# Attention and a gated feed-forward layer on one core: the q, k, v loads change queue, the fallback path is rewritten, the last two output tiles change engine

## The chip, the cores and the metric

The kernel runs on one core of a Trainium2 chip. The core has a matrix engine (TensorE, PE in the profile), three elementwise engines (VectorE or DVE, ScalarE or ACT, GpSimd or POOL) and a sync engine (SyncE, SP) that issues transfers. Each engine works through its own list of instructions in order, and semaphores tie the lists together. Transfers between device memory and the on-chip buffers run on 16 shared DMA engines; an engine that issues one puts it on its own queue (SP's, ACT's, or POOL's, which the profile calls q1, q10 and q0). The metric is the device time of one execution in microseconds (us).

## The reference

Eight batches with eight heads, 1152 keys and a head size of 64. Queries are averaged in pairs, so that there are 576 of them per head; then comes ordinary softmax attention. Its 4608 x 512 result goes through a feed-forward layer in which two projections are multiplied:

```
q_pool = q.reshape(B, H, S // 2, 2, D).mean(axis=3)
attn   = softmax(q_pool @ k^T / sqrt(D))
x      = (attn @ v)            # to 4608 x 512
out    = ((x @ w1) * (x @ w2)) @ w3 @ w_out
```

## The kernel before

**Staging.** The 64 heads are handled as 32 pairs `p` (two heads share the 128 partitions). For each pair, k, q and v are loaded as float32 (`load_kq`, lines 206 to 209, and `load_v`, lines 211 to 215), POOL casts k and v and adds neighbouring queries (`cast_kq`, `cast_v`, lines 228 to 236), and the cast block `kq16` is transposed into `kqT`: on PE for pairs 0 to 7 (`transp_pe`), by a transposing transfer on SP's queue from pair 8 on (`transp`, line 243). `kst`, `qst`, `qtl` and `vst`, the landing buffers, have two copies each, `kq16` two, `kqT` three, `vaugs` six.

**Attention.** `scores(s)` computes 512 columns of the scores of both heads on PE (line 301), and ACT takes the exponential into a ring buffer (line 306). No maximum is subtracted. `av_unit` multiplies 128 query rows with v (line 363), DVE takes the reciprocal of the sum and scales (lines 368, 375), and the result goes to `xT`, transposed on PE for early pairs and by a transfer on SP's queue for pairs from 8 on (`x_dma`, line 320).

**Feed-forward.** `w3 @ w_out` is formed once. Chunks of 512 rows of `xT` go through steps `a` and `b` (lines 459, 472, 474) and `o` (line 453), which gives an output tile `osb` of 128 x 512 (three buffers). While attention still runs, DVE scales that tile and POOL's queue stores it (line 483). After the last score (`tail`), DVE scales the first half and ACT the second, and SP stores it (lines 478 to 480). The next to last tile goes to ACT's queue. The last tile is made in two column halves by `fill_last` (lines 497 to 510): DVE scales the first, ACT the second, and ACT's queue stores both.

**What sets the order.** The string `PLAN` is the order of PE's work, written out by hand: `s` a score slot, `a` and `c` units of attention times v, `f`, `F` and `D` feed-forward steps, `k`, `j` and `t` transposes. The other engines' lists follow from it. When the scores reach a new pair `pn`, `slot` (lines 587 to 600) issues the transposing transfer of pair `pn + 1` and `prepare(pn + 2)`: POOL casts k and q of that pair, casts v of the pair before it, and then come the loads of v of that pair and of k and q of the pair two later. `eng` in line 574 says from which queue: POOL's below pair 8, SP's from there on. Since queues are served in order, whatever waits at the head of POOL's list (a store waiting for its tile, say) holds the casts behind it, and whatever waits at the head of SP's list (an `x_dma` waiting for DVE, a load waiting for its buffer) holds the transposes behind it.

**The fallback.** As no maximum is subtracted, the kernel counts reciprocal sums that are out of bounds (`count_bad`, `read_bad`). All engines read that count (line 668) and branch on it (line 670): if it is not zero, `_general` computes everything again in a plain loop over batches. With the given inputs it is zero and every engine jumps over that code to its end, but the code is there in each engine's list: the loop's body is unrolled over the heads.

Of the kernel before, what the change touches and what calls it, by code (L numbers as in the profile page):

```python
# [8 lines left out]
FP32 = mybir.dt.float32  # L9
FP16 = mybir.dt.float16  # L10
AF = mybir.ActivationFunctionType
ALU = mybir.AluOpType
# [14 lines left out]
def _general(tc, q, k, v, out, w1sb, w2sb, T16):  # L27

    nc = tc.nc
    B, H, S, D = q.shape  # L30
    Sq = S // 2
    NJ = S // 128
    dm = H * D
# [8 lines left out]
    kf, qf, vf = (t.rearrange("b h s d -> (b h) s d") for t in (k, q, v))  # L42
    with tc.tile_pool(name="gen", bufs=1) as sb, \
         tc.tile_pool(name="gen_ps", bufs=1, space=bass.MemoryType.PSUM) as ps, \
         tc.For_i(0, B, 1) as ib:
        xT = sb.tile([128, NC, Sq], FP16)
        for h in range(H):
            ih = ib * H + h
            hs = (h % 2) * 64
            kst = sb.tile([128, NJ, D], FP32, tag="g_kst")  # L50
            nc.sync.dma_start(out=kst, in_=kf[bass.ds(ih, 1)].rearrange("o (c p) d -> p (o c) d", p=128))
            vst = sb.tile([128, NJ, D], FP32, tag="g_vst")
            nc.sync.dma_start(out=vst, in_=vf[bass.ds(ih, 1)].rearrange("o (c p) d -> p (o c) d", p=128))
            qst = sb.tile([QP, QC, 2, D], FP32, tag="g_qst")
            nc.sync.dma_start(out=qst, in_=qf[bass.ds(ih, 1)].rearrange("o (c p t) d -> p (o c) t d", p=QP, t=2))
            kh = sb.tile([128, NJ, 128], FP16, tag="g_kh")
            qh = sb.tile([QP, QC, 128], FP16, tag="g_qh")
            vh = sb.tile([128, NJ, D], FP16, tag="g_vh")
            nc.vector.memset(kh, 0.0)
            nc.vector.memset(qh, 0.0)  # L60
            nc.vector.tensor_copy(out=kh[:, :, 0:D], in_=kst)
            nc.vector.tensor_tensor(out=qh[:, :, 0:D], in0=qst[:, :, 0, :], in1=qst[:, :, 1, :], op=ALU.add)
            nc.vector.tensor_copy(out=vh, in_=vst)
            kT = sb.tile([128, NJ, 128], FP16, tag="g_kT")
            nc.sync.dma_start(out=kT, in_=kh.rearrange("p c d -> p (c d)"), transpose=True)
            qT = sb.tile([128, QC, QP], FP16, tag="g_qT")
            nc.sync.dma_start(out=qT, in_=qh.rearrange("p c d -> p (c d)"), transpose=True)
            kTf = kT.rearrange("p c i -> p (c i)")
            pav = ps.tile([128, 1024], FP32, tag="g_pav")
            for c in range(QC):  # L70
                pss = ps.tile([128, S // W, 512], FP32, tag="g_pss")
                for w in range(S // W):
                    nc.tensor.matmul(pss[0:QP, w, 0:W], qT[:, c, :], kTf[:, w * W:w * W + W], start=True, stop=True)
# [4 lines left out]
                e = sb.tile([QP, S // W, W], FP32, tag="g_e")  # L78
# [6 lines left out]
                eh = sb.tile([QP, S], FP16, tag="g_eh")  # L85
                nc.vector.tensor_scalar(out=eh, in0=e.rearrange("p w i -> p (w i)"), scalar1=rz, scalar2=SCL,
                                        op0=ALU.mult, op1=ALU.mult)
                eT = sb.tile([128, NJ, QP], FP16, tag="g_eT")
                nc.sync.dma_start(out=eT, in_=eh, transpose=True)
                pc = pav[hs:hs + 64, (c // 5) * 512 + (c % 5) * QP:(c // 5) * 512 + (c % 5) * QP + QP]  # L90
                for jt in range(NJ):
                    nc.tensor.matmul(pc, vh[:, jt, :], eT[:, jt, :], start=(jt == 0), stop=(jt == NJ - 1))
                nc.vector.tensor_copy(out=xT[hs:hs + 64, h // 2, c * QP:c * QP + QP], in_=pc)
# [24 lines left out]
def kernel(  # L118
# [11 lines left out]
    nc = tc.nc  # L130

    B, H, S, D = q.shape
    Sq = S // 2
    NJ = S // 128
# [4 lines left out]
    HP = H // 2  # L139
# [9 lines left out]
    SCL = 16.0  # L149
# [7 lines left out]
    CH = 512  # L157
# [304 lines left out]
    def put(step, pt):  # L462
        kind, c, ft = step
        tail = st["s"] == NS
        if kind == "turn":
            w3T[ft] = msb.tile([128, NF, 128], FP16, tag="w3T", bufs=2, name="w3T")
            nc.vector.tensor_copy(out=w3T[ft].rearrange("p a i -> p (a i)"), in_=pt.bitcast(FP16))
        elif kind == "mult":
            nc.vector.tensor_copy(out=T16[:, ft, :], in_=pt)
        elif kind == "a":  # L470
            asbs[ft] = msb.tile([128, CH], FP32, tag="asb", bufs=2, name="asb")
            (nc.scalar.copy if tail else nc.vector.tensor_copy)(out=asbs[ft], in_=pt)  # L472
# [24 lines left out]
    def fill_last():  # L497
        _, c, n = take()
        osb = msb.tile([128, dm], FP32, tag="osb", bufs=3, name="osb")
        for x in range(2):  # L500
            cs = slice(x * 256, x * 256 + 256)
            pt = double()[:, 0, 0:256]
            for f_ in range(NF):
                nc.tensor.matmul(pt, gTs[c][:, f_, n * 128:n * 128 + 128], T16[:, f_, cs],
                                 start=(f_ == 0), stop=(f_ == NF - 1))
            if x == 0:
                nc.vector.tensor_scalar_mul(out=osb[:, cs], in0=pt, scalar1=1.0 / (SCL * SCL))
            else:
                nc.scalar.mul(out=osb[:, cs], in_=pt, mul=1.0 / (SCL * SCL))
            store(nc.scalar, c * CH + n * 128, osb, cs)  # L510

    def fill_two(banks):
        st["mode"] = 1
# [188 lines left out]
```

## Time and profile before

| what | us |
|---|---|
| median of three runs | 414.12 (414.11 to 414.66) |
| the profiled execution | 416.36 |
| its span, first to last instruction | 414.6 |
| PE busy | 397.8 |
| ACT busy | 323.9 |
| DVE busy | 207.0 |
| POOL busy | 164.6 |

The time of the profiled execution holds 1.76 us outside the span. Busy time counts computing instructions of an engine, and for POOL the making of its transfers. A group row names the line, the engine, what is written and read, how often, the busy time and the mean duration of one in ns; the releaser is what ended the idle time before it. `POOLq`, `SPq` and so on are the sequencers of these engines.

### The profile page before, as it was taken

How to read it: one execution, taken by the hardware profiler on the slowest of the kernel's cores; microseconds unless marked ns; L12 is line 12 of the kernel's file. 1: busy time of each engine (PE TensorE's matmuls, PEld its weight loads, DVE VectorE, ACT ScalarE, POOL GpSimd, SP SyncE). 2: the span in 40 equal slices, each digit the busy share in tenths (PEclk: the TensorE clock that was granted, in tenths of full speed). 3: DMA queues.
4: the chain of work that ended last, by engine and by line, in shares of the span. 5: the costliest groups of instructions: out<-in, count | busy, mean ns of one | idle time of the engine just before them, and what ended most of it. 6: DMA issues, size and time to landing. Idle time of an engine off the chain costs nothing.

```text
span 414.6 us, 12630 instructions
## 1 busy us (share of the span) xinstructions
PE 397.8 (96%) x5273; PEld 233.3 (56%) x5273; DVE 207.0 (50%) x568; ACT 323.9 (78%) x357; POOL 164.6 (40%) x208
## 2 busy tenths in 40 slices
PE   4889999999999999999999999999999999999993
PEld 1547665656456655555556545565687555654442
DVE  2446555656356544564455635554466366454331
ACT  4878988999989999999888898998888977323231
POOL 2879977653173317530564057304443200000000
PEclk9999999999999999999999999999999999999998
DMA  8999999999989959999899989894995622120303
GB/s 262 226 321 278 267 283 307 350 253 272 279 189 237 265 179 239 306 270 262 217 222 281 280 218 296 228 233 95 258 262 115 173 52 15 40 86 4 103 0 108
DMA packets 91359, 86.34 MB, mean 208 GB/s; under 512 B 59680, under 2 KB 65056, under 8 KB 91296
## 3 DMA queue, kind: packets, MB, share of 16 engines
q1 hardware_dynamic: 82000, 59.78, 59.8%
q0 software_dynamic: 8720, 25.10, 21.6%
q8 instruction: 43, 0.70, 0.7%
q10 hardware_dynamic: 576, 0.59, 0.4%
q14 instruction: 20, 0.16, 0.2%
HBM read 67.11 MB, written 9.44 MB: 185 GB/s over the span
## 4 chain that ended last, share of the span: by engine, by line
PE 91%; DMA 6%; DVE 0%; POOL 0%; issue 0%; SPq 0%; ACT 0%; ACTq 0%; DVEq 0%; POOLq 0%
PE one L459 22%; PE psc L301 19%; PE one L363 18%; PE one L453 12%; PE psc L459 9%; PE one L450 3%; PE psc L453 3%; DMA w3c<-in_moe_w_dram 3%; PE one L390 3%; DMA wosb<-in_moe_w_out_dram 2%; DMA kst<-in_k_dram 1%; PE psc L248 1%; PE one L447 1%; PE one L331 0%; PE one L328 0%
## 5 line engine op out<-in xcount | busy, mean ns | idle before, releaser
L306 ACT ACTIVATE ring<-psc 128x1024 f16<-128x1024 f32 x324 | 307.2, 1027 | 41.7 <-PE psc L301 40.9
L301 PE MATMUL psc<-kqT 64*128 64x512 f16 (+7 forms) x1152 | 95.3, 290 | 1.3 <-DVE kqT L251 0.7
L363 PEld LDWEIGHTS <-ring 128*128 128x128 f16 x2304 | 81.2, 98 | 26.4 <-issue 11.4
L363 PE MATMUL one<-vaug,ring 128*128 128x65 f16 x2304 | 90.6, 194 | 0.0
L301 PEld LDWEIGHTS <-kqT 64*128 64x128 f16 x1152 | 43.8, 95 | 39.5 <-issue 20.2
L225 POOL CAST kq<-kst 128x1152 f16<-128x1152 f32 x31 | 35.7, 1152 | 52.3 <-DMA kqT<-kq 31.6
L459 PE MATMUL one<-xT,w1sb 128*128 128x512 f16 (+1 forms) x224 | 53.6, 364 | 0.0
L453 PE MATMUL one<-T,gT 128*128 128x512 f16 x224 | 53.0, 380 | 0.0
L459 PE MATMUL one<-xT,w2sb 128*128 128x512 f16 (+1 forms) x224 | 51.5, 357 | 0.0
L472 DVE COPY asb<-one 128x512 f32<-128x512 f32 x46 | 31.8, 692 | 26.4 <-PE one L459 26.4
L474 DVE TENSOR_TENSOR gT<-one,asb 128x512 f16<-128x512 f32 x50 | 34.6, 692 | 20.7 <-PE one L459 18.6
L430 POOL DMA_DIRECT2D out_dram<-osb x21 | 11.6, 554 | 82.4 <-DVE rzall L368 50.1
L459 PEld LDWEIGHTS <-w2sb 128*128 128x128 f16 x320 | 28.5, 97 | 26.2 <-issue 1.8
L453 PEld LDWEIGHTS <-gT 128*128 128x128 f16 x280 | 25.3, 98 | 31.4 <-issue 4.6
L459 PEld LDWEIGHTS <-w1sb 128*128 128x128 f16 x320 | 27.5, 97 | 25.8 <-issue 3.7
L368 DVE RECIPROCAL rzall<-one 128x2 f32<-128x2 f32 x128 | 21.4, 167 | 40.2 <-PE one L363 29.3
L219 POOL TENSOR_TENSOR kq<-qst 128x512 f16<-128x512 f32 x30 | 38.2, 1273 | 3.3 <-DMA qst<-in_q_dram 3.3
L482 DVE TENSOR_SCALAR osb<-one 128x512 f32<-128x512 f32 x24 | 16.6, 692 | 42.8 <-PE one L453 42.8
L236 POOL CAST vaug<-vst 128x1152 f16<-128x1152 f32 x32 | 36.6, 1144 | 3.1 <-DMA vst<-in_v_dram 3.0
L375 DVE TENSOR_TENSOR xb<-one,rzall 128x128 f16<-128x128 f32 x96 | 28.0, 292 | 3.3
L474 DVE TENSOR_TENSOR gT<-psc,asb 128x512 f16<-128x512 f32 x22 | 15.2, 692 | 15.0 <-ACT asb L472 9.3
L459 PE MATMUL psc<-xT,w2sb 128*128 128x512 f16 (+1 forms) x96 | 22.6, 361 | 0.0
(78 smaller groups left out, 257.0 us busy)
## 6 DMA issues: line engine op xcount, KB each, us to landing
vst<-in_v_dram SPq DMA_DIRECT2D x25, 576.0 KB, 5.3
kst<-in_k_dram SPq DMA_DIRECT2D x23, 576.0 KB, 5.9
qst<-in_q_dram SPq DMA_DIRECT2D x23, 512.0 KB, 6.9
out_dram<-osb POOLq DMA_DIRECT2D x21, 256.0 KB, 5.1
kst<-in_k_dram POOLq DMA_DIRECT2D x8, 576.0 KB, 9.9
qst<-in_q_dram POOLq DMA_DIRECT2D x8, 512.0 KB, 11.2
vst<-in_v_dram POOLq DMA_DIRECT2D x7, 576.0 KB, 7.0
out_dram<-osb SPq DMA_DIRECT2D x9, 256.0 KB, 2.0
```

The lines of the kernel that those rows point to most:

```text
L219: eng.tensor_tensor(out=kq16[:, NJ:NJ + QM].rearrange("p c u d -> p u c d"), in0=qv[:, :, :, 0], in1=qv[:, :, :, 1], op=ALU.add)
L225: nc.gpsimd.tensor_copy(out=kq16[:, 0:NJ].rearrange("p c u d -> p u c d"), in_=kq[p][0])
L236: nc.gpsimd.tensor_copy(out=va[:, :, :, 0:D], in_=vs.pop(p).rearrange("p u (c d) -> p u c d", d=D))
L301: nc.tensor.matmul(psc[:, u, f - s * G:f - s * G + ln], kT2[u * 64:u * 64 + 64, jt, :], qpT[u * 64:u * 64 + 64, i0:i0 + ln], start=True, s ...
L306: nc.scalar.activation(out=ring[:, :, r0:r0 + G], in_=psc, func=AF.Exp, bias=0.0, scale=SCALE)
L363: nc.tensor.matmul(one[:, u * E1:u * E1 + E1], ring[:, u, c0:c0 + 128], va[:, u, jt, :], start=(jt == 0 and u == 0), stop=(jt == NJ - 1), ...
L368: nc.vector.reciprocal(out=rz, in_=av[:, :, D:E1].rearrange("p u o -> p (u o)"))
L375: nc.vector.tensor_tensor(out=xbt, in0=av[:, :, 0:D], in1=rz.unsqueeze(2).to_broadcast([128, 2, D]), op=ALU.mult)
L453: nc.tensor.matmul(pt, gTs[c][:, f_, ft * 128:ft * 128 + 128], T16[:, f_, :], start=(f_ == 0), stop=(f_ == NF - 1))
L459: nc.tensor.matmul(pt[:, d0:d0 + n], wt[:, mc, ft * 128:ft * 128 + 128], xT[:, mc, a:a + n], start=(mc == 0 and d0 == 0), stop=(mc == NC - ...
L472: (nc.scalar.copy if tail else nc.vector.tensor_copy)(out=asbs[ft], in_=pt)
L474: nc.vector.tensor_tensor(out=gTs[c][:, ft, :], in0=pt, in1=asbs.pop(ft), op=ALU.mult)
```

## The change

1. `prepare` takes POOL's queue for the loads of v, k and q of every pair, except v of pair 20, which stays on SP's queue. SP's list keeps the first loads, the transposes and stores at the end.
2. In the tail, the next to last tile is scaled by ACT alone in one 128 x 512 instruction and stored from SP's queue. The last tile has both halves scaled by ACT; the first is stored from SP's queue, the second from ACT's.
3. `_general` loads a whole batch at once, packs two heads into the 128 partitions instead of padding with zeros, and transposes a head's six query blocks in one transfer instead of six. It still isn't executed with these inputs. SP's list, the whole program counted, goes from 255 to 93 rows, DVE's from 951 to 880, ACT's from 40 to 38 (repeated ones in a row counted once), POOL's from 208 to 297; PE's has 12060 in both. Of these the part after the branch, which holds the fallback, has 103 rows before and 28 after on SP, 417 and 348 on DVE; on ACT it holds 48 exponentials both times.

`PLAN` is unchanged. The diff, cut:

```
     def prepare(p):
         cast_kq(p)
         cast_v(p - 1)
-        eng = nc.gpsimd if p < 8 else nc.sync
-        load_v(p, eng)
+        eng = nc.gpsimd
+        load_v(p, nc.sync if p == 20 else eng)
...
             osb = msb.tile([128, dm], FP32, tag="osb", bufs=3, name="osb")
-            if tail:
+            if tail and st["f"] >= len(steps) - 1:
+                nc.scalar.mul(out=osb, in_=pt, mul=1.0 / (SCL * SCL))
+                store(nc.sync, c * CH + ft * 128, osb)
+            elif tail:
                 nc.vector.tensor_scalar_mul(out=osb[:, 0:256], in0=pt[:, 0:256], scalar1=1.0 / (SCL * SCL))
                 nc.scalar.mul(out=osb[:, 256:512], in_=pt[:, 256:512], mul=1.0 / (SCL * SCL))
-                store(nc.scalar if st["f"] >= len(steps) - 1 else nc.sync, c * CH + ft * 128, osb)
+                store(nc.sync, c * CH + ft * 128, osb)
...
-            if x == 0:
-                nc.vector.tensor_scalar_mul(out=osb[:, cs], in0=pt, scalar1=1.0 / (SCL * SCL))
-            else:
-                nc.scalar.mul(out=osb[:, cs], in_=pt, mul=1.0 / (SCL * SCL))
-            store(nc.scalar, c * CH + n * 128, osb, cs)
+            nc.scalar.mul(out=osb[:, cs], in_=pt, mul=1.0 / (SCL * SCL))
+            store((nc.sync, nc.scalar)[x], c * CH + n * 128, osb, cs)
...
 _general:
-            kst = sb.tile([128, NJ, D], FP32, tag="g_kst")
-            nc.sync.dma_start(out=kst, in_=kf[bass.ds(ih, 1)].rearrange("o (c p) d -> p (o c) d", p=128))
+        kst = sb.tile([128, H, NJ * D], FP32, tag="g_kst")
+        nc.sync.dma_start(out=kst, in_=kf[bass.ds(ib, 1)].rearrange("o (x p c) d -> p (o x) (c d)", p=128, c=NJ))
...
-                eT = sb.tile([128, NJ, QP], FP16, tag="g_eT")
-                nc.sync.dma_start(out=eT, in_=eh, transpose=True)
+            eT = sb.tile([128, QC * NJ, QP], FP16, tag="g_eT")
+            nc.sync.dma_start(out=eT, in_=eh.rearrange("p c s -> p (c s)"), transpose=True)
```

More of the change, by code (lines that the diff above doesn't have):

```diff
@@ L41, in _general @@
     W = 384
-    kf, qf, vf = (t.rearrange("b h s d -> (b h) s d") for t in (k, q, v))
+    NW = S // W
+    kf, qf, vf = (t.rearrange("b h s d -> b (h s) d") for t in (k, q, v))
     with tc.tile_pool(name="gen", bufs=1) as sb, \
@@ new lines, in _general @@
+        kst = sb.tile([128, H, NJ * D], FP32, tag="g_kst")
+        nc.sync.dma_start(out=kst, in_=kf[bass.ds(ib, 1)].rearrange("o (x p c) d -> p (o x) (c d)", p=128, c=NJ))
+        vst = sb.tile([128, H, NJ * D], FP32, tag="g_vst")
+        nc.sync.dma_start(out=vst, in_=vf[bass.ds(ib, 1)].rearrange("o (x p c) d -> p (o x) (c d)", p=128, c=NJ))
+        qst = sb.tile([QP, H * QC, 2 * D], FP32, tag="g_qst")
+        nc.sync.dma_start(out=qst, in_=qf[bass.ds(ib, 1)].rearrange("o (c p t) d -> p (o c) (t d)", p=QP, t=2))
@@ new lines, in _general @@
+        kh = sb.tile([128, HP, NJ, 2, D], FP16, tag="g_kh")
+        qh = sb.tile([QP, HP, QC, 2, D], FP16, tag="g_qh")
+        vh = sb.tile([128, H * NJ, D], FP16, tag="g_vh")
+        kv_ = kst.rearrange("p (x u) (c d) -> p x u c d", x=HP, d=D)
+        qv = qst.rearrange("p (x u c) d -> p x u c d", x=HP, u=2)
+        for u in range(2):
+            nc.vector.tensor_copy(out=kh[:, :, :, u, :], in_=kv_[:, :, u])
+            nc.vector.tensor_tensor(out=qh[:, :, :, u, :], in0=qv[:, :, u, :, 0:D], in1=qv[:, :, u, :, D:2 * D], op=ALU.add)
@@ new lines, in _general @@
+        nc.vector.tensor_copy(out=vh, in_=vst.rearrange("p h (c d) -> p (h c) d", d=D))
+        kT = sb.tile([128, HP * NJ, 128], FP16, tag="g_kT")
+        nc.sync.dma_start(out=kT, in_=kh.rearrange("p x c u d -> p (x c u d)"), transpose=True)
+        qT = sb.tile([128, HP * QC, QP], FP16, tag="g_qT")
+        nc.sync.dma_start(out=qT, in_=qh.rearrange("p x c u d -> p (x c u d)"), transpose=True)
+        pav = ps.tile([128, 1024], FP32, tag="g_pav")
+        for h in range(H):
+            hp, hs = h // 2, slice((h % 2) * 64, (h % 2) * 64 + 64)
+            eh = sb.tile([QP, QC, S], FP16, tag="g_eh")
+            for c in range(QC):
+                pss = ps.tile([128, NW, 512], FP32, tag="g_pss")
+                for w in range(NW):
+                    t0 = hp * NJ + w * (NJ // NW)
+                    nc.tensor.matmul(pss[0:QP, w, 0:W], qT[hs, hp * QC + c, :],
+                                     kT[hs, t0:t0 + NJ // NW, :].rearrange("p c i -> p (c i)"), start=True, stop=True)
@@ L77, in _general @@
                 nc.vector.tensor_scalar_mul(out=nb, in0=mx, scalar1=-SCALE)
[L78 removed]
+                e = sb.tile([QP, NW, W], FP32, tag="g_e")
                 nc.scalar.activation(out=e, in_=pss[0:QP, :, 0:W], func=AF.Exp, bias=nb, scale=SCALE)
@@ L84, in _general @@
                 nc.vector.reciprocal(out=rz, in_=z)
[L85 to L86 removed]
+                nc.vector.tensor_scalar(out=eh[:, c, :], in0=e.rearrange("p w i -> p (w i)"), scalar1=rz, scalar2=SCL,
                                         op0=ALU.mult, op1=ALU.mult)
[L88 to L90 removed]
+            eT = sb.tile([128, QC * NJ, QP], FP16, tag="g_eT")
+            nc.sync.dma_start(out=eT, in_=eh.rearrange("p c s -> p (c s)"), transpose=True)
+            for c in range(QC):
+                pc = pav[hs, (c // 5) * 512 + (c % 5) * QP:(c // 5) * 512 + (c % 5) * QP + QP]
                 for jt in range(NJ):
[L92 to L93 removed]
+                    nc.tensor.matmul(pc, vh[:, h * NJ + jt, :], eT[:, c * NJ + jt, :], start=(jt == 0), stop=(jt == NJ - 1))
+            for c0, c1 in ((0, 5), (5, QC)):
+                nc.vector.tensor_copy(out=xT[hs, hp, c0 * QP:c1 * QP], in_=pav[hs, (c0 // 5) * 512:(c0 // 5) * 512 + (c1 - c0) * QP])
         gT = sb.tile([128, NF, Sq], FP16)
```

24 lines of the change are left out of this document (1 added, 23 removed).

## The prediction

> **What bounds the kernel.** I read the page first, then the busy time by stretches, then the chain of waits at the end. Of the page, the span, PE's line, and the shares of the chain that ended last:
>
> ```profile
> span 414.6 us, 12630 instructions
> PE 397.8 (96%) x5273; PEld 233.3 (56%) x5273; DVE 207.0 (50%) x568; ACT 323.9 (78%) x357; POOL 164.6 (40%) x208
> PE 91%; DMA 6%; DVE 0%; POOL 0%; issue 0%; SPq 0%; ACT 0%; ACTq 0%; DVEq 0%; POOLq 0%
> ```
>
> An average of 96% hides where the other 4% are. The view by stretches tells (length; busy time of each engine; clock, DMA share, GB/s):
>
> ```profile
> 0.00:10.00 10.00, 3.86 (x26) 1.69 (x26) 1.80 (x6) 4.59 (x7) 2.72 (x11) 1.00 0.81 259
> 20.00:40.00 20.00, 18.16 (x303) 11.78 (x300) 10.35 (x37) 16.71 (x19) 16.80 (x23) 1.00 1.03 311
> 60.00:80.00 20.00, 20.00 (x303) 12.33 (x301) 11.68 (x36) 18.07 (x20) 14.98 (x20) 1.00 0.98 321
> 200.00:220.00 20.00, 20.00 (x299) 11.90 (x295) 10.76 (x30) 17.52 (x19) 11.37 (x14) 1.00 1.15 224
> 380.00:400.00 20.00, 20.00 (x95) 8.98 (x93) 6.65 (x13) 5.58 (x12) 0.00 (x0) 1.00 0.16 53
> 408.00:414.60 6.60, 0.29 (x3) 0.01 (x1) 0.00 (x0) 0.38 (x1) 0.00 (x0) 0.69 0.28 89
> ```
>
> PE is idle in the ramp, where the change moves nothing (`prepare` used POOL's queue there already), and in the last 6.3 us. Between, in the stretch where the loads change queue, PE has no idle time to give back: 20.00 of 20.00 at full clock. So moving the loads can't gain; it can only cost, or free something at the end. What can gain is the tail. Its rows: the chain, ACT's timeline, and the transfers' own times to landing (the SP rows are the stores issued at 403.99 and 405.7, the ACT rows those at 407.45, 407.97 and 408.82):
>
> ```profile
> 404.81 1.73 PE one L453 x8
> 406.54 0.89 PE psc L504 x8
> 407.97 0.34 ACTq L430
> 408.41 0.38 ACT osb L509
> ```
>
> ```profile
> 407.45 0.85 ACTq L430 DMA_DIRECT2D out_dram<-osb  x2
> 408.41 0.38 ACT L509 ACTIVATE osb<-psc 128x256 f32<-128x256 f32 x1 [0.99 <-PE psc L504]
> 408.82 0.88 ACTq L430 DMA_DIRECT2D out_dram<-osb  x1
> ```
>
> ```profile
> out_dram<-osb SPq DMA_DIRECT2D x1, 256.0 KB, 2.1
> ...
> out_dram<-osb SPq DMA_DIRECT2D x1, 256.0 KB, 2.2
> ...
> out_dram<-osb ACTq DMA_DIRECT2D x1, 256.0 KB, 3.4
> out_dram<-osb ACTq DMA_DIRECT2D x1, 128.0 KB, 3.2
> out_dram<-osb ACTq DMA_DIRECT2D x1, 128.0 KB, 3.5
> ```
>
> PE's last matmul ends at about 408.29 (the 408.00 stretch shows 0.29 us of PE). ACT starts the last scaling at 408.41, issues its store at 408.82, and the store lands 3.5 us later, at 412.3. Here are the instructions of the branch over the fallback, by sequencer:
>
> ```profile
> L670 SPq EVENT_SEMAPHORE  x8: 17/17/17, 412.3 to 412.9; - x8
> L670 PEldq COMPARE_BRANCH  x1: 4282/4282/4282, 406.6 to 406.6; - x1
> L670 SPq COMPARE_BRANCH  x1: 58/58/58, 407.0 to 407.0; - x1
> L670 DVEq COMPARE_BRANCH  x1: 72/72/72, 408.2 to 408.2; - x1
> L670 ACTq COMPARE_BRANCH  x1: 62/62/62, 410.3 to 410.3; - x1
> L670 ACTq EVENT_SEMAPHORE  x1: 17/17/17, 410.8 to 410.8; - x1
> L670 DVEq EVENT_SEMAPHORE  x1: 21/21/21, 412.3 to 412.3; - x1
> ```
>
> SP's closing waits begin at 412.3, when the last store lands, and the rest to 414.6 (2.3 us) is the closing sequence. So the tail is: PE's end 408.29, plus 0.12 until ACT starts, 0.38 of scaling, 0.03 to the issue, 3.5 to the landing, 2.3 to close.
>
> **The change, part by part.**
>
> *Loads to POOL's queue.* 23 loads of v (pairs 8 to 31 without 20) and 22 each of k, q and the q remainder (pairs 10 to 31) go from SP's list to POOL's: 89 transfers. The price of one on POOL, from the eight pairs that already did so, and what POOL waits for longest:
>
> ```profile
> L208 POOL DMA_DIRECT2D kst<-in_k_dram x8: 712/728/746, 12.0 to 71.5; - x8
> L202 POOL DMA_DIRECT2D qst<-in_q_dram x8: 724/724/729, 12.7 to 72.2; - x8
> L203 POOL DMA_DIRECT2D qtl<-in_q_dram x8: 607/607/613, 13.4 to 72.9; - x8
> L214 POOL DMA_DIRECT2D vst<-in_v_dram x7: 726/726/726, 14.0 to 70.8; - x7
> POOL out_dram L430 <- DVE rzall L368: 50.1, 9, 17.3
> ```
>
> One `prepare` gets 0.728 + 0.724 + 0.607 + 0.726 = 2.79 us longer; over all, 23 x 0.726 + 22 x 2.059 = 62 us, so POOL goes from 164.6 to about 227 us, 55% of the span. That is beside PE's work as long as POOL catches up before the next transpose needs its cast. The cover is POOL's waiting at stores: nine waits of 50.1 us in total, one of 17.3 us, each ending when PE finishes an output tile, whatever POOL did before. In the stretch 60 to 80, where POOL issues these loads now, it is 14.98 of 20 us busy and PE does not stop. I take zero. The lower bound is zero as well, since PE has no idle time there. The upper bound comes from the transposes that have least room. For the pairs 15 and 20: issue, us to landing, and PE's group that holds the pair's first score:
>
> ```profile
> 156.18 1.54 SPq L243 DMA_TRANSPOSE kqT<-kq  x1
> kqT<-kq SPq DMA_TRANSPOSE x1, 7.3
> 164.88 0.83 PE L301 MATMUL psc<-kqT 64*128 64x384 f16 x10
> ...
> 203.06 4.41 SPq L243 DMA_TRANSPOSE kqT<-kq  x1
> kqT<-kq SPq DMA_TRANSPOSE x1, 11.6
> 216.67 0.83 PE L301 MATMUL psc<-kqT 64*128 64x128 f16 x12
> ```
>
> They land at 163.5 and 214.7 and are read from 164.9 and 216.7: 1.4 and 2.0 us of room. One `prepare` of delay in front of such a transpose would cost 2.79 - 1.4 = 1.4 us; two that weren't caught up, 5.58 - 2.0 = 3.6 us. Pair 15's transpose is held by PE's own progress (an `x_dma` sits ahead of it), not by POOL. Pair 20's k is cast right after POOL's long wait at a store, ahead of the new loads, so the delay doesn't reach it either. What the transposes gain is that no loads stand ahead of them on SP's queue: 203.06 follows three loads there. A store behind four loads on POOL's queue gets about 2.8 us later; its tile buffer is reused three tiles on, and tiles come over 3 us apart, so that is covered too. Against it speaks one rule. The Trainium skill (SBUF — State Buffer, Who interferes with whom) says that a POOL-issued transfer can't write its descriptors while DVE holds the shared port, so that such loads should stay on a hardware queue. By that rule the 89 issues would stretch; the rows above have 712 to 746 ns for k, in a stretch where DVE was busy 11.68 of 20 us, and show none of it.
>
> *The tail.* The next to last tile: one ACT instruction over 128 x 512. The trace has a copy of that size on ACT:
>
> ```profile
> 399.67 0.59 ACT L472 COPY asb<-psc 128x512 f32<-128x512 f32 x1 [2.00 <-PE psc L459]
> ```
>
> PE ends that tile at 406.54, so ACT is done by about 407.2 and SP stores it. The first half follows at 407.43 + 0.04 + 0.38 = 407.9, again stored by SP. Both cost nothing on the path. ACT no longer issues two stores (0.85 us) ahead of the last scaling, which can start 0.04 us after PE's end, at 408.33 instead of 408.41: 0.08 us saved. The last store is then the only one on ACT's queue. What it needs to land is the unknown: between the 2.0 to 2.2 us of SP's rows, undisturbed 256 KB stores, and the 3.5 us that it takes now, third in its queue and with an issue of 0.88 instead of 0.34. It is half the size of SP's and first on its queue, so I stand nearer to SP's: 2.4 us. The end: 408.33 + 0.38 + 0.03 + 2.4 + 2.3 = 413.44, against 414.6: 1.16 us less.
>
> *The short fallback.* Never executed. Where it could show is the jump over it: ACT, with a short body, goes on 0.5 us after its branch (410.3 to 410.8), DVE only after 4.1 us (408.2 to 412.3). SP's jump gets short like ACT's. Now it is hidden behind the landing; I take zero, with the rival below for the other end. The Trainium skill (Runtime: NRT & Kernel Launch, Instruction fetch mechanics) says that a taken branch beyond the prefetched window waits for a transfer of code. DVE's 4.1 us and ACT's 0.5 agree with it.
>
> **The sum** is made against the profiled execution: 416.36 - 1.16 = 415.20. The median of the runs is 2.24 us below that execution, and I take the difference over: 414.12 - 1.16 = 413.0.
>
> **The rivals.**
>
> *The tail's gain stays small.* If the last store keeps ACT's 3.2 to 3.5 us, because they belong to the queue and not to the crowd in it, the gain is 0.08 to 0.4 us: 413.7 to 414.0. For it: all three ACT stores took 3.2 to 3.5, the first one too. Against it: the three overlapped each other.
>
> *SP comes late to its end (slower).* SP now issues a store at 407.9 that ACT issued before, and it branches 1.3 us after its last store (405.7 to 407.0 now), so at 409.2. If its jump still took DVE's 4.1 us, it would go on at 413.3 instead of 412.3: 1.0 us slower, 415.1. This decides once the jump takes over 3.1 us. Against it: SP's fallback shrinks from 103 rows to 28 (repeats in a row counted once), which hold fewer instructions than ACT's 48 exponentials and go the way of ACT's 0.5 us.
>
> *POOL falls behind.* If two `prepare`s of delay reach a transpose with 2.0 us of room, PE loses 3.6 us, the tail gives 1.16 back: 416.6. The net is a loss once more than 3.2 us of delay reach it. The starved descriptors of the rule above would end here. Against it: the 60 to 80 stretch.
>
> **How the numbers follow.** A measurement of this kernel tells about 0.2%, 0.83 us, from no change: below 413.29 is faster, above 414.95 slower. The tail gains as summed: 0.55, time 413.0, own range 412.5 (landing in 2.0) to 413.3. The small gain: 0.27, 413.7 to 414.0, within the bound. SP late: 0.07, 415.1. POOL behind: 0.11, 416.6. That gives 0.55 faster, 0.27 same, 0.18 slower. The range reaches from 412.3 (2.0 us to landing, less 0.2 us for the spread of runs) to 415.1, and leaves out POOL's case and little else.
>
> **What would show it.** Right: PE still 20.00 of 20.00 in all stretches from 60 to 400, its last matmul at 408.3; POOL near 227 us; SP's closing waits from about 411.2; the last ACT store landing in about 2.4 us, with an issue near 0.35. Wrong: PE idle before a score group with `kqT` as releaser; POOL issues far over 0.75 us; the last store at 3.2 us or more; SP's closing waits well after that landing.

## The result and the profile after

| what | before, us | after, us |
|---|---|---|
| median | 414.39 (414.11 to 415.25, 4 runs) | 456.11 (449.16 to 463.7, 4 runs) |
| the profiled execution | 416.36 | 456.36 |
| its span | 414.6 | 454.5 |

The changed kernel takes 1.0918 times as long (95% interval 1.0872 to 1.0964): 9% slower, far outside the predicted range. Ratios, here and below, compare only executions within 1.5% of the fastest of their kernel, while medians are over all of them. The executions of after spread over 15 us where those of before spread over 1 us, so a few us between two kernels that lose time in this way say little. What is quoted is one execution near the middle.

The page of the profile of after: its span and busy times, and the chain that ended last, by engine and by line:

```profile
span 454.5 us, 12511 instructions
...
PE 409.3 (90%) x5273; PEld 238.9 (53%) x5273; DVE 206.3 (45%) x566; ACT 324.9 (71%) x358; POOL 225.3 (50%) x297
...
PE 58%; DMA 33%; POOL 4%; issue 3%; DVE 0%; SPq 0%; ACT 0%; POOLq 0%
DMA kqT<-kq 25%; PE one L464 12%; PE psc L306 11%; PE one L368 11%; PE one L458 8%; PE psc L464 6%; DMA qst<-in_q_dram 5%; PE one L455 3%; PE psc L458 3%; PE one L395 1%; DMA kst<-in_k_dram 1%; PE psc L253 1%; POOL kq L224 1%; DMA vst<-in_v_dram 1%; POOL vaug L241 1%
```

The chain was PE for 91% before. Now a quarter of it is one kind of transfer, the transpose of a pair's k and q into `kqT`. (Line numbers of after are five higher from `transp` on: L243 is L248, L301 is L306.) POOL is busy 225.3 us, as summed in advance (227), so POOL is not the surprise. The view by stretches of after, with the columns of the prediction's:

```profile
60.00:80.00 20.00, 20.00 (x267) 11.73 (x266) 11.74 (x33) 17.64 (x20) 17.18 (x23) 1.00 0.96 284
200.00:220.00 20.00, 15.75 (x191) 8.48 (x190) 6.08 (x16) 11.83 (x13) 9.97 (x14) 0.91 1.11 184
280.00:300.00 20.00, 9.12 (x162) 5.52 (x160) 5.65 (x17) 9.79 (x11) 3.44 (x6) 0.78 1.12 175
320.00:340.00 20.00, 15.40 (x210) 10.97 (x208) 8.28 (x20) 14.21 (x15) 8.81 (x12) 0.97 1.19 180
340.00:360.00 20.00, 15.69 (x240) 12.18 (x241) 7.74 (x22) 10.04 (x11) 9.13 (x10) 0.77 0.93 132
```

While the transposes are still PE's (60 to 80), nothing is lost. Later PE stands idle up to half of a stretch, and between 200 and 340 the three stretches shown have a DMA share of 1.1 to 1.2 while they move only 175 to 184 GB/s, where 200 to 220 had 224 before. The clock of 0.77 to 0.78 is an average over 20 us: it mixes full clock with spells at 0.50, one of which is this:

```profile
299.80:304.90 5.10, 5.10 (x32) 2.23 (x34) 1.15 (x3) 1.02 (x1) 5.03 (x6) 0.50 0.67 104
```

What the waits of after are (us in total, times, longest):

```profile
POOL kq L230 <- DMA kqT<-kq: 56.8, 9, 16.6
...
PE psc L306 <- DMA kqT<-kq: 27.8, 5, 10.9
```

PE waits for `kqT` five times, 27.8 us. That is two thirds of the loss. (POOL, too, waits for it for 56.8 us, where 31.6 us were spent so before.) The records of the matmuls give the account: the last one ends at 449.50 instead of 408.29, 41.2 us later. Idle time of PE after 20 us rises from 2.7 to 32.2 us, which is 29.5 of it (the longest stops are 288.9 to 299.8 and 335.4 to 344.1); the other 11.7 us are matmuls that take longer, as PE's busy time says too (409.3 - 397.8 = 11.5). The clock accounts for them: after 20 us the trace of after has six spells at 0.50, each behind or within a stop of PE of 1.8 to 11 us, and PE works 23.8 us in them; a 128 x 512 matmul follows the one before it after 427 ns there instead of 216, so about half of 23.8, 11.9 us, is lost. The trace of before has no such spell while PE works. The end, from the last matmul to the end of the span, is 5.0 us instead of 6.3.

Why `kqT` is late stands in the view of transfers, 100 to 340 us. First before (queue: packets, MB, share of 16 engines; then issues, KB each, median us to landing):

```profile
q1 hardware_dynamic: 69433, 47.42, 83.7%
q0 software_dynamic: 1968, 6.29, 9.2%
...
vst<-in_v_dram SPq DMA_DIRECT2D x20, 576.0 KB, 5.3
kst<-in_k_dram SPq DMA_DIRECT2D x18, 576.0 KB, 5.8
...
kqT<-kq SPq DMA_TRANSPOSE x21, 7.2
xT<-xb SPq DMA_TRANSPOSE x21, 5.1
```

And the same of after:

```profile
q0 software_dynamic: 10092, 37.39, 61.2%
q1 hardware_dynamic: 44194, 11.54, 42.7%
...
kst<-in_k_dram POOLq DMA_DIRECT2D x19, 576.0 KB, 10.2
vst<-in_v_dram POOLq DMA_DIRECT2D x17, 576.0 KB, 7.1
...
kqT<-kq SPq DMA_TRANSPOSE x19, 13.8
...
xT<-xb SPq DMA_TRANSPOSE x18, 10.3
```

The transposes, on SP's queue with a single load now, land in 13.8 us instead of 7.2, and the `x` transposes in 10.3 instead of 5.1. One case in full. SP's timeline of after (start, us of issuing), the transfer's own time to landing, and PE's group that waits for it:

```profile
273.92 6.07 SPq L248 DMA_TRANSPOSE kqT<-kq  x1
```

```profile
kqT<-kq SPq DMA_TRANSPOSE x1, 25.8
```

```profile
299.80 0.55 PE L306 MATMUL psc<-kqT 64*128 64x448 f16 x2 [10.88 <-DMA kqT<-kq]
```

It was issued 15 us before PE came to it at 288.9, and lands 25.8 us after its issue. Beside it POOL's timeline has the loads of other pairs:

```profile
269.95 0.74 POOL L219 DMA_DIRECT2D vst<-in_v_dram  x1
...
273.37 0.74 POOL L213 DMA_DIRECT2D kst<-in_k_dram  x1 [2.68 <-DMA kst<-in_k_dram]
...
280.54 0.73 POOL L219 DMA_DIRECT2D vst<-in_v_dram  x1
281.26 0.72 POOL L213 DMA_DIRECT2D kst<-in_k_dram  x1
```

In before, the same transfers stood in one line on SP's queue:

```profile
225.13 3.64 SPq L243 DMA_TRANSPOSE kqT<-kq  x1
228.86 0.53 SPq L214 DMA_DIRECT2D vst<-in_v_dram  x1
229.49 0.41 SPq L208 DMA_DIRECT2D kst<-in_k_dram  x1
230.00 0.42 SPq L202 DMA_DIRECT2D qst<-in_q_dram  x1
```

The packet records show that one line being served in order. Until 227 the loads of the preparation before still move some 380 KB per us, and no transpose packet starts; then the transposes run nearly alone (635 packets in the microsecond from 228, 1086 in the next); from 231 on the new loads, which are needed much later, move over 320 KB per us. So a transpose does wait for loads ahead of it and is left alone by those behind it. In the case of after both run at once, from 289 to 298: 26 to 80 transpose packets start per us while POOL's queue moves 45 to 322 KB. In the microsecond from 300, in which POOL's queue moves nothing, 1049 start. The packet records of both traces, 90 to 360 us (each microsecond in which a transpose packet starts counts):

```
                                  before              after
transpose packet, 256 B           27 ns, median 18    37 ns, median 18
load packet                       2304 B: 123 ns,     4608 B: 300 ns,
                                    median 93           median 186
microseconds with transposes      130                 216
transpose packets started in one  408                 213
  while POOL's queue moves
    60 to 200 KB                                      188 (94 of them)
    200 KB or more                                    86 (59 of them)
```

The loads' packets are twice as large from POOL's queue, and by the median a byte takes as long in either; the means are longer because some packets took many times the median. A transpose gets half as many packets per microsecond as before, and a fifth beside loads at full rate. The Trainium skill (DMA: Bandwidth & Descriptors, SWDGE vs HWDGE vs iDMA) says that software and hardware queues feed different internal queues of a DMA engine, which takes turns between them and changes over at packet boundaries. The trace agrees: in the 59 microseconds with loads at full rate, 86 transpose packets start beside 66 load packets, not far from one for one.

The same records split a landing in two. From issue to the first of its 1792 packets, a `kqT` transpose of before takes 1.2 to 1.4 us with no load ahead of it, and up to 6.8 us with 1.6 MB ahead. From its first packet to its last it takes 1.8 to 3.7 us where under 150 KB of other queues run beside it (18 of 21 between 100 and 340 us). In after the second part is 2.1 to 2.5 us for the four with under 100 KB beside them, and 5.8 to 16.8 us for the seven with over 1 MB. The first part is then long as well, up to 18 us with no load ahead, because the transposes before are still at it.

So the trace of before had the price too, on a small scale, for POOL's queue stores output tiles there. Pair 20's transpose, issued at 203.06, is the slowest to land; it takes 6.4 us from its first packet to its last, beside 0.6 MB of them. POOL's queue from its issue to its landing:

```profile
q0 software_dynamic: 240, 0.79, 37.6%
```

### The profile page after: what moved, and what is told of

Same layout as the page of the kernel before. It is cut to its first block, busy times and chain, and to the rows that moved or that the text cites. A ratio compares the mean times of both kernels' runs of the same rounds, so it can differ in the third digit from the quotient of the medians.

```text
span 454.5 us, 12511 instructions
## 1 busy us (share of the span) xinstructions
PE 409.3 (90%) x5273; PEld 238.9 (53%) x5273; DVE 206.3 (45%) x566; ACT 324.9 (71%) x358; POOL 225.3 (50%) x297
## 4 chain that ended last, share of the span: by engine, by line
PE 58%; DMA 33%; POOL 4%; issue 3%; DVE 0%; SPq 0%; ACT 0%; POOLq 0%
DMA kqT<-kq 25%; PE one L464 12%; PE psc L306 11%; PE one L368 11%; PE one L458 8%; PE psc L464 6%; DMA qst<-in_q_dram 5%; PE one L455 3%; PE psc L458 3%; PE one L395 1%; DMA kst<-in_k_dram 1%; PE psc L253 1%; POOL kq L224 1%; DMA vst<-in_v_dram 1%; POOL vaug L241 1%
## 5 line engine op out<-in xcount | busy, mean ns | idle before, releaser
L306 PE MATMUL psc<-kqT 64*128 64x512 f16 (+7 forms) x1152 | 98.1, 294 | 29.3 <-DMA kqT<-kq 27.8
L368 PEld LDWEIGHTS <-ring 128*128 128x128 f16 x2304 | 85.0, 100 | 28.3 <-issue 13.4
L368 PE MATMUL one<-vaug,ring 128*128 128x65 f16 x2304 | 94.4, 197 | 0.0
L306 PEld LDWEIGHTS <-kqT 64*128 64x128 f16 x1152 | 44.1, 96 | 69.7 <-DMA kqT<-kq 29.1
L230 POOL CAST kq<-kst 128x1152 f16<-128x1152 f32 x31 | 35.7, 1152 | 60.7 <-DMA kqT<-kq 56.8
L458 PE MATMUL one<-T,gT 128*128 128x512 f16 x224 | 54.6, 388 | 1.4 <-issue 1.4
L464 PE MATMUL one<-xT,w1sb 128*128 128x512 f16 (+1 forms) x224 | 55.2, 373 | 0.0
L479 DVE TENSOR_TENSOR gT<-one,asb 128x512 f16<-128x512 f32 x50 | 34.5, 691 | 21.9 <-PE one L464 19.9
L207 POOL DMA_DIRECT2D qst<-in_q_dram x30 | 21.7, 723 | 3.9 <-DMA kst<-in_k_dram 2.8
L213 POOL DMA_DIRECT2D kst<-in_k_dram x30 | 21.8, 727 | 3.3 <-DMA kst<-in_k_dram 2.7
```

The costliest lines, as they stand in the source:

```text
L213: k_eng.dma_start(out=kst, in_=k_view(p))
L230: nc.gpsimd.tensor_copy(out=kq16[:, 0:NJ].rearrange("p c u d -> p u c d"), in_=kq[p][0])
L306: nc.tensor.matmul(psc[:, u, f - s * G:f - s * G + ln], kT2[u * 64:u * 64 + 64, jt, :], qpT[u * 64:u * 64 + 64, i0:i0 + ln], start=True, s ...
L368: nc.tensor.matmul(one[:, u * E1:u * E1 + E1], ring[:, u, c0:c0 + 128], va[:, u, jt, :], start=(jt == 0 and u == 0), stop=(jt == NJ - 1), ...
L458: nc.tensor.matmul(pt, gTs[c][:, f_, ft * 128:ft * 128 + 128], T16[:, f_, :], start=(f_ == 0), stop=(f_ == NF - 1))
L464: nc.tensor.matmul(pt[:, d0:d0 + n], wt[:, mc, ft * 128:ft * 128 + 128], xT[:, mc, a:a + n], start=(mc == 0 and d0 == 0), stop=(mc == NC - ...
```

## The experiments

The theories: the loss comes from **sharing** (transposes beside loads of another queue on full DMA engines); from **POOL's time** (its 62 us of issuing make casts, and so transposes, late); from the **circle** (a late transpose holds the cast block, which holds POOL, whose list holds the next cast); and, of the change's parts, from the loads or from tail and fallback.

### The tail alone

Before, with the changed tail (the diff of the last two tiles above).

> The kernel before with the new tail alone; loads and fallback as before. If the tail works as the changed kernel's end shows it (PE's last matmul to the end of the span 5.0 us instead of 6.3), the time falls by about 1.2 us, ratio 0.997, whatever theory holds for the loads. If the long fallback on SP keeps SP from its closing waits (a jump that takes about 4 us after its branch, as DVE's did), the gain shrinks or turns into a loss of up to 1 us.

Measured: 414.75 us (12 runs) against 414.33 (29 runs); ratio 1.0021 (1.0003 to 1.0039). The predicted gain of 1.16 us (0.9972) is excluded. The last store did land sooner than before's 3.5 us:

```profile
out_dram<-osb ACTq DMA_DIRECT2D x1, 128.0 KB, 2.7
```

But SP, with the long fallback, goes on only 3.0 us after its branch, 0.7 us after that store has landed:

```profile
L670 SPq EVENT_SEMAPHORE  x8: 17/17/17, 409.9 to 410.5; - x8
...
L670 SPq COMPARE_BRANCH  x1: 58/58/58, 406.9 to 406.9; - x1
```

### The loads alone

```
-        eng = nc.gpsimd if p < 8 else nc.sync
-        load_v(p, eng)
+        eng = nc.gpsimd
+        load_v(p, nc.sync if p == 20 else eng)
```

> The kernel before with the loads moved to POOL's queue alone. Every theory that puts the loss on the loads: 450 to 465 us, ratio about 1.10, kqT transposes landing in about 13 us. If the rewritten fallback or the tail had a part in the loss (code loading), clearly less than that.

Measured: 452.88 us (445.72 to 454.46, 4 runs) against 414.33, 38.5 us of the 41.7; what is left lies within the spread of such kernels. `kqT` lands in 4.0/9.8/25.4 us, with a median below the 13 us that was expected and a maximum like that of after. Its row of 100 to 340 us and its last two stores, on the old tail:

```profile
100.00:340.00 240.00, 212.81 (x2945) 123.85 (x2942) 106.51 (x291) 186.28 (x197) 137.08 (x173) 0.94 1.02 205
```

```profile
out_dram<-osb ACTq DMA_DIRECT2D x2, 128.0 KB, 2.6
```

PE loses 27 of 240 us. The row of the stores is the median of two, 2.9 and 2.4 us. Over the 12 traces with the old tail the last store lands in 1.9 to 3.5 us, 2.4 in the median: the 3.5 us on which the prediction built its gain is the longest of them.

### Tail and fallback, the loads as before

> The changed kernel with the loads left where they were. 413.0 us, ratio 0.997; PE without gaps from 60 to 400 us and kqT transposes landing in about 7 us as before. If the fallback's length matters at the end, this is faster than the tail alone by up to 1 us; else the same.

Measured: 414.41 us (12 runs); ratio 1.0005 (0.999 to 1.0021); `kqT` lands in 4.0/7.4/11.4 us (min/median/max; before 4.0/7.2/11.6, after 4.0/13.4/26.5). The short fallback costs nothing, and neither does the tail; together they don't gain the 1.2 us that were expected. SP's closing waits begin at 410.00 here, right with the landing of the last store at 409.98, so the short fallback removes the 0.7 us by which SP was late with the tail alone; the times of the two kernels, 0.3 us apart, are too close to tell that. In 100 to 340 us PE is busy for 239.87 of 240 us, at a DMA share of 0.92.

### POOL's issues without the loads

The loads stay on SP's queue, and POOL issues four tiny transfers in each `prepare` from pair 8 on, at the place of the loads.

```
+        if p >= 8:
+            for i in range(4 if p + 2 < NP else 1):
+                tiny = att.tile([128, 2, 4], FP32, tag="tiny", bufs=4)
+                nc.gpsimd.dma_start(out=tiny, in_=v[0, 0:2, 0:128, 4*i:4*i+4]...)
```

> The kernel before with its loads on SP's queue, and beside them four tiny transfers (256 pieces of 16 bytes each) on POOL's queue where the changed kernel has its loads, so that POOL spends about 2.5 us more in each of its preparations and moves nearly no bytes. Theory A (transposes and loads share the 16 DMA engines from two queues, and the transposes are what suffers): no change within 1%, kqT landing in about 7 us. Theory B (POOL comes late with its casts, so the transposes start late): most of the loss is back, 440 to 455 us.

Measured: 415.28 us (10 runs); ratio 1.005 (1.002 to 1.0079); `kqT` 4.1/8.0/14.4. The group of POOL's issues (count, busy us, mean ns, idle before):

```profile
L579 POOL DMA_DIRECT2D tiny<-in_v_dram x90 | 64.8, 722 | 6.6 <-DMA tiny<-in_v_dram 5.4 <-DMA kqT<-kq 0.9 <-issue 0.3
```

The same time on POOL's list (64.8 us, 228.4 busy in all) costs half a per cent, not nine. POOL's time falls as the cause. The predicted zero for it was nearly right.

### A soft order: loads wait for the previous pair's transpose

POOL reads four columns of `kqT` of pair `p - 1` ahead of its loads, so that it issues them only when that transpose has landed.

```
+        if p > NPE:
+            gate = att.tile([128, 4], FP16, tag="gate", bufs=2)
+            nc.gpsimd.tensor_copy(out=gate, in_=pairs[p - 1][1][:, 0:4])
         load_v(p, nc.sync if p == 20 else eng)
```

> The loads on POOL's queue, but before issuing them POOL copies four columns of the transposed block of the pair before, so that it can't run ahead: its loads leave only when that transposing transfer has landed. Theory A (packets of loads from a second queue alternate with the small packets of the transposes): far fewer loads beside each transpose, so kqT lands clearly sooner than the 9.8 us of the loads-only kernel and most of the loss goes, below 430 us. If software-made transfers are just slower whenever they run: no change, about 450 us. If POOL's lateness were the cause: worse, above 450 us, since POOL now waits more.

Measured: 439.95 us (434.39 to 447.5, 4 runs); ratio 1.0503 (1.046 to 1.0546); `kqT` 4.2/9.3/16.8. About a third of the 38.5 us that the loads alone cost comes back, less than expected. The longest landing falls from 25.4 to 16.8 us, the median hardly (9.8 to 9.3).

### A part of the loads on POOL's queue

Only v (a third of the bytes), and only k and q:

```
-        load_v(p, eng)
+        load_v(p, nc.gpsimd)
```

```
-        eng = nc.gpsimd if p < 8 else nc.sync
-        load_v(p, eng)
+        eng = nc.gpsimd
+        load_v(p, nc.gpsimd if p < 8 else nc.sync)
```

> Only v's loads (24 of them) on POOL's queue, k and q stay on SP's. A third of the moved bytes. Theory A: the loss grows with the bytes beside the transposes, so about a third of 38 us or less, since the slack of a few us absorbs the first delays: 416 to 428 us, kqT landing at 8 to 10 us.

> k's and q's loads on POOL's queue, v's on SP's. Two thirds of the moved bytes. Theory A: two thirds of the loss or more, 430 to 450 us, kqT landing at 9 to 11 us. Both this and the v-only kernel near 414 us would mean that it isn't the bytes beside the transposes but all loads being out of SP's order.

Measured: v 436.13 us (426.37 to 438.45, 4 runs) against 414.82, `kqT` 4.1/13.1/18.5; k and q 440.99 us (426.58 to 460.78), ratio 1.0348 (1.0279 to 1.0417), `kqT` 4.0/11.3/28.6. By the medians each part alone brings half of the loss or more; by the lowest times, which are equal for the two, 12 us of 31. A third of the bytes does as much there as two thirds, so the loss isn't in proportion to the bytes. For v the time, at 436, and the landing, at 13.1, lie above what was expected. The kernel with v alone also has a loss of its own: POOL waits 73.9 us for v itself, where it waits 6.7 in after. What that costs is open.

### One transfer per head

```
-    eng.dma_start(out=vst, in_=v[b, h0:h0 + 2]...)
+    for u in range(2):
+        eng.dma_start(out=vst[:, u], in_=v[b, h0 + u]...)      # k and q likewise
```

> Loads on POOL's queue as in the loads-only kernel, but one transfer per head, so that the two pieces of 2304 bytes of a partition can't be joined: the trace of the changed kernel shows packets of 4096 and 4608 bytes on POOL's queue (243 and 300 ns each) and 2048 and 2304 bytes on SP's (91 and 123 ns). If the packets' size sets how long a transpose's 256-byte packet waits for its turn: packets near 2304 bytes, kqT landing sooner than 9.8 us and a good part of the loss gone, 420 to 440 us, although POOL issues six transfers a pair instead of four (about 2 us more). If the size doesn't matter: 450 us or more.

Measured: 472.85 us (463.04 to 488.37); ratio 1.1222 (1.1156 to 1.1288); `kqT` 4.2/10.6/36.1. The packets stayed at 4096 and 4608 bytes, so this says nothing of packet size. It has more issues and is slower still.

### A strict order: loads only when the newest transpose has landed

The same gate, but in `slot`, right behind `transp(pn + 1)` and on its `kqT`; the loads follow the gate, one pair later than in after.

```
                 transp(pn + 1)
+                gate = att.tile([128, 4], FP16, tag="gate", bufs=2)
+                nc.gpsimd.tensor_copy(out=gate, in_=pairs[pn + 1][1][:, 0:4])
+                loads_of(pn + 1)
```

> The loads on POOL's queue, issued only after the newest transposing transfer has landed (the gate now reads the block whose transpose was issued just before), and ahead of the next casts. This is the order that SP's single queue gave, but made on POOL. Theory A: transposes run nearly alone again, kqT at 5 to 8 us, and the time is near the kernel before, 414 to 422 us. If loads by POOL are worse in themselves: still 440 us or more.

Measured: 435.12 us (430.69 to 439.25); ratio 1.0414 (1.0331 to 1.0497). The transposes land in 4.0/5.9/8.7 us, better than before: running beside the loads is what made them late, since the queue, the packets and the bytes are those of after. The time did not follow, for the gate is a wait of its own. Its waits, of POOL first and then of SP's queue:

```profile
POOL gate L600 <- DMA kqT<-kq: 97.9, 22, 6.1
```

```profile
SPq L243 <- POOL vaug L236: 166.1, 23, 12.2
```

```profile
100.00:340.00 240.00, 223.89 (x3147) 133.84 (x3144) 114.34 (x311) 196.29 (x207) 147.72 (x202) 0.98 0.88 218
```

POOL waits 97.9 us for landings, its casts come late, SP waits for them with the next transposes (166.1 us), and the DMA engines are less full (0.88). PE still loses 16 of 240 us; its waits for `kqT` are 7.4 us in the whole run, and the cause of the rest stays open. While POOL holds the order in this way it can't cast. SP's one queue held it for nothing.

### The loads on ACT's queue

```
-        eng = nc.gpsimd if p < 8 else nc.sync
+        eng = nc.gpsimd if p < 8 else nc.scalar
```

> The loads on ACT's queue instead of POOL's: also a second queue beside SP's transposes, but made by hardware and in packets like SP's. ACT pays some 1.7 to 3 us a pair for issuing them and waits for POOL's casts in between, so the time says little (I expect 430 to 470 us); what tells is the transposes' landing. If a second queue of any kind is enough: kqT at 10 us or more. If the software queue with its 4096 and 4608 byte packets is needed: kqT near 7 us.

Measured: 474.38 us (469.97 to 476.14); ratio 1.1415 (1.1315 to 1.1515); `kqT` 3.9/5.9/17.1. This says little of the queue: what ACT's list waits for at a load (a buffer, a cast) holds its exponentials, and few loads ran beside transposes (between 100 and 340 us, 8 of 33 MB in microseconds in which transpose packets start; in after 27 of 37 MB of POOL's queue). The waits show who is late:

```profile
PE psc L301 <- ACT ring L306: 33.6, 27, 5.0
```

### A third cast block

The circle opened: three copies of `kq16` instead of two (and five `vaugs`, for the room), with the loads on POOL's queue.

> The loads-only kernel with three cast blocks instead of two (and five v blocks instead of six, to make room), so that POOL's cast of k needs the transpose of three pairs ago instead of two. If the loss is a circle (late transpose, so late cast, so late next transpose): POOL's wait for kqT (40.6 us in the loads-only kernel) goes and with it more than half of the loss, 415 to 430 us. If the transposes' own slowness is what counts: 440 us or more.

Measured: 466.13 us (452.11 to 478.27). POOL's wait for `kqT` is gone, PE's is not, `kqT` lands in 4.1/13.8/31.1 us, and the time is no better. The circle falls as the cause of the late transposes. (POOL now waits for its loads instead, 24.6 us for k and 22.1 for v.)

```profile
PE psc L301 <- DMA kqT<-kq: 26.4, 4, 16.2
```

### The same queue, fewer bytes

The loads on POOL's queue, each v of pair 8 and up cut to a ninth; the casts read that part repeatedly.

```
+        n = NJ * D if p < 8 else D
+        eng.dma_start(out=vst[:, :, 0:n], in_=v[...][:, :, 0:n])
```

> The loads-only kernel in which v of pairs from 8 on is loaded to a ninth only (64 of 576 numbers a row, the cast reads them nine times over), so the result isn't the reference's. A third of the moved bytes is gone, the count of transfers and POOL's instructions are the same. Theory A with DMA engines that are nearly full in the kernel before (93% of the stretch from 100 to 340 us): the transposes' waits shrink and the time falls to 414 to 425 us. If the order of the queues alone were the cause, whatever the bytes: 440 us or more.

Measured: 417.77 us (417.56 to 422.47); ratio 1.0114 (1.0026 to 1.0202); `kqT` 4.0/7.4/19.9. As many issues on POOL as after, k and q beside the transposes as after, and the loss is nearly gone once the DMA engines have room (0.85). With k and q on POOL's queue and all of v moved from SP's, above, it was 3.5%. The stretch:

```profile
100.00:340.00 240.00, 237.62 (x3385) 142.31 (x3384) 121.82 (x332) 211.16 (x223) 143.47 (x181) 0.99 0.85 176
```

### Only v, on a second hardware queue

```
-        load_v(p, eng)
+        load_v(p, nc.gpsimd if p < 8 else nc.scalar)
```

> Only v's loads on ACT's queue, k and q on SP's: the pair of the kernel with v on POOL's queue (436.1 us, kqT at 13.1 us), with a second queue made by hardware and packets as on SP's. v's buffer was freed one preparation earlier, so ACT should not wait for POOL; 24 issues of about 0.4 us, some 10 us of ACT's idle time. If a second queue of any kind beside the transposes is enough: kqT at 10 us or more and 425 to 440 us. If the software queue with its packets of 4096 and 4608 bytes is what hurts: kqT at 7 to 8.5 us and 414 to 420 us.

Measured: 423.02 us (421.54 to 426.42, 4 runs) against 413.72; ratio 1.0252 (1.0195 to 1.0308); `kqT` 4.2/8.0/17.7. By the medians the same v loads cost 9 us from ACT's queue and 21 us from POOL's; the lowest time from POOL's queue, 426.37, is as high as the highest from ACT's, 426.42. The views of transfers, 100 to 340 us, of v on ACT's queue and then on POOL's:

```profile
vst<-in_v_dram ACTq DMA_DIRECT2D x21, 576.0 KB, 5.8
...
kqT<-kq SPq DMA_TRANSPOSE x21, 6.9
```

```profile
vst<-in_v_dram POOLq DMA_DIRECT2D x22, 576.0 KB, 8.5
...
kqT<-kq SPq DMA_TRANSPOSE x20, 13.1
```

The two medians are not of like cases: with v on ACT's queue 6 of 21 transposes have more than 250 KB of other queues beside their own packets, with v on POOL's 10 of 19. Those that do are slow in both. Beside 0.6 to 0.7 MB, two transposes take 5.2 and 5.8 us from first packet to last with v on ACT's queue, and five take 6.6 to 8.6 with v on POOL's; beside 0.9 MB, one of each takes 12.2 and 6.9; beside under 100 KB it is 1.7 to 3.7 and 1.9 to 3.4. So loads on a second hardware queue slow a transpose too. Whether POOL's slow it more, by their larger packets or by the kind of queue, stays open: the cases are few, and no run here changed one without the other. How much of the 9 us comes from sharing and how much from ACT's list being held is open as well.

No version was faster than before.

## Why the prediction was wrong

- **"I take zero. The lower bound is zero as well" (the loads): the failed step.** It counted what the 89 transfers cost POOL, and nothing of what the queue does for the order in which they run. The price of an issue was right (722 to 724 ns in the median for k, q and v), so was POOL's total, and the issues alone cost half a per cent (tiny transfers). What was left out is the landing of the transposes: 7.2 to 13.8 us in the median, 11.6 to 26.5 at most, where 1.4 to 2.0 us of room had been found. PE waits 27.8 us for them and loses 11.9 us more at half clock. The room was the right place to look. The delay was sought only ahead of the transfer, not in it.
- **"What the transposes gain is that no loads stand ahead of them on SP's queue".** There was such a wait, up to 6.8 us before a first packet, and it went; but loads behind a transpose on its own queue leave it alone, and loads on another queue run beside it, which cost more than the wait. With the order forced, landing fell to 5.9 us. For pair 20, "203.06 follows three loads there" was half of the reading: POOL's stores ran beside that transpose.
- **What was quoted and not read.** The prediction's stretches between 20 and 220 have a DMA share of 0.98 to 1.15. Zero was argued from the stretch 60 to 80, where POOL already loaded and PE did not stop; but there PE makes the transposes itself, and no small transfer is waited for. It was evidence for POOL's issuing only. The run with fewer bytes shows that the room counts: with k and q still on POOL's queue, the loss shrinks to 1.1% at a share of 0.85.
- **The rival "POOL falls behind"** had the sign and the releaser (`kqT`), and neither the mechanism nor the size: 2.5 us were allowed for, 42 came. POOL did wait longer (56.8 us for `kqT` against 31.6), as a result of late transposes. The starved descriptors of that rival did not show: 0.71 to 0.74 us per issue of k, q and v with DVE at half load.
- **The tail's 1.16 us** was mis-sized. The mechanism was there: ACT's last store issues in 0.36 us and lands in 2.7 to 2.8 us (2.4 were summed), one 128 x 512 scaling takes 0.60 us, each half 0.38. But the old tail's last store lands in 1.9 to 3.5 us, 2.4 in the median of 12 traces, and a single row of 3.5 was taken for the price. The tail's rows of after:

```profile
447.79 0.60 ACT L483 ACTIVATE osb<-one 128x512 f32<-128x512 f32 x1 [0.88 <-PE one L458]
...
449.54 0.38 ACT L514 ACTIVATE osb<-psc 128x256 f32<-128x256 f32 x1 [0.44 <-PE psc L512]
449.95 0.36 ACTq L435 DMA_DIRECT2D out_dram<-osb  x1
```

```profile
out_dram<-osb ACTq DMA_DIRECT2D x1, 128.0 KB, 2.8
```

- **The short fallback at zero** was right for the time, and SP goes on half a us after its branch, as ACT did. The rival "SP comes late" was real with the long fallback: 3.0 us, and 0.7 us late with the tail alone. The rows of after:

```profile
L675 SPq EVENT_SEMAPHORE  x8: 17/17/17, 450.9 to 452.8; - x8
L675 SPq COMPARE_BRANCH  x1: 58/58/58, 450.4 to 450.4; - x1
```

**What is shown and what is argued.** Shown: the loads bring the loss, and the tail and the fallback none of it; two thirds of it are PE's waits for `kqT`, most of the rest matmuls at half clock behind the stops; POOL's issuing time and the cast blocks are not the cause; order or fewer bytes restore the landing, and fewer bytes the time as well. Argued from the packet records: that the engines' turns between queues are the means. Open: the part of the larger packets, and what the strict order still loses.

## What to carry to other kernels

Where the DMA share of a stretch is near 1, a queue is also an order: transfers with little room and bulk loads for later belong on one queue, the urgent one first, and moving the bulk to a free queue takes that order away. Before calling a moved load hidden, list the transfers that will now run beside it, and hold their landing times, not their issue times, against the room of those who wait. Where the trace of before already has a case of such sharing, as with POOL's stores here, read the price there. Take a price that varies between executions, such as a last store's landing, from more than one row.

## What was not expected of the hardware

- A load of the same size and shape goes out in packets of 2048 and 2304 bytes from SP's queue and of 4096 and 4608 bytes from POOL's, at 84 and 93 ns, and 167 and 186 ns, in the median.
- With the loads on POOL's queue the DMA engines were busier and moved less than with the loads on SP's: 206 GB/s at a share of 1.05 against 226 at 0.94. The view of the stretch 100 to 340, before and then after:

```profile
100.00:340.00 240.00, 239.87 (x3451) 143.52 (x3444) 124.88 (x340) 214.14 (x226) 93.48 (x108) 1.00 0.94 226
```

```profile
100.00:340.00 240.00, 214.72 (x2957) 124.32 (x2954) 108.33 (x295) 188.26 (x199) 132.47 (x168) 0.95 1.05 206
```

  The Trainium skill (DMA: Bandwidth & Descriptors, Issuing engines are not separate DMA queues) says that issuing from several engines saves only the issuing engine's time, all transfers running interleaved on the same engines. Here it also cost the transposes twice their landing time. The GB/s follow the slower kernel as well, so they don't tell by themselves what the engines could have moved.
- Of the 41 us, 12 are slower matmuls and not waiting: with stops of PE from 1.8 us up came spells of 3.4 to 13.7 us at a granted clock of 0.50 (a stop of 1.4 us in the same trace brought none). Such a wait cost more than its length.
